# A planned attention-and-FFN kernel: new due times and engines for its copies, and slack and a lead in its plan

## The chip, the cores and the metric

One core of a Trainium2 chip runs the whole program. The metric is the device time of one execution in microseconds; lower is better. Three executions of the kernel before took 958.62, 960.18 and 961.11 us (median 960.18).

## The reference

Eight batches of eight heads, 576 positions, head size 64: causal attention over a window of 64 keys, softmax in fp32, its heads laid side by side into rows of 512; then two matrix products with a softplus between them.

```python
scores = scale * np.matmul(q, k.transpose(0, 1, 3, 2))
mask = (rel >= 0) & (rel < window)              # rel = query - key, window = 64
scores = np.where(mask, scores, -1000000000.0)
scores = scores - np.max(scores, axis=-1, keepdims=True)
attn = np.exp(scores)
attn = attn / (np.sum(attn, axis=-1, keepdims=True) + 1e-09)
x = np.matmul(attn, v)                          # -> rows of 4608 tokens x 512
...
h = x @ w_in                                    # 512 x 2048
g = np.maximum(h, 0.0) + np.log1p(np.exp(-np.abs(h)))
out = g @ w_out                                 # 2048 x 512
```

`w_in` and `w_out` come as 64-bit words, so the kernel turns them into a high and a low 32-bit part itself.

## The kernel before, in words

The 4608 tokens are cut into 12 blocks of 384 (`TB`). For each block g there are four attentions, one for each pair of heads hp (`attention(g, hp)`), and 16 FFN steps, one for each 128 columns f of the hidden layer (`ffn`). A step is an "up" (12 matmuls of 384 columns into `ps_h`, line 711), a softplus (ScalarE: Abs, Exp, Ln, lines 715 to 717; VectorE: line 723), a split of the result into a high part (line 725, on ScalarE or VectorE) and a low part (line 726, VectorE), and a "down" (9 matmuls of 512 columns that add into `ps_o`, line 735). `ps_h` and `u` have two buffers each. The steps run in a fixed order: block 0 with f = 0 to 7, block 1 with all 16, block 0 with f = 8 to 15, then blocks 2 to 11; what block 0 has summed halfway goes to DRAM and is added later.

Each f needs its weights converted once (`convert(f)`): a load of 1024 KB (line 348), "abs" on ScalarE (350), two shifts on VectorE (352, 353), a copy "hi" on ScalarE (355), and a subtraction "lo" on VectorE (356).

An attention is a chain: loads of q and k (lines 404, 405, or 435 and 439), scores on TensorE (416, or 468 and 470), a masked minimum on VectorE (389), six exponentials with sums on ScalarE (496), the reciprocal (504, 505) and the normalizing on VectorE (511). In blocks 0 and 1 the weights are then turned on TensorE (547), copied (550), multiplied with v (558) and copied and split into `x` (564, 565); from block 2 on they are split into bf16 parts (595 to 600), turned by DMA (591), multiplied (658) and gathered (665 to 670). Blocks 0 and 1 take q, k from four slots (`q_two`, `k_two`, `qk_far`) and v from `v_two`.

No engine's order is written by hand. Every operation is put in a list by `add` with its engine, a cost in us, what it depends on and what buffers it opens; `arrange` is a list scheduler in Python: again and again it takes the engine that can start earliest and there, of the operations that could start then, the one with the smallest due time. The program issues the operations in that order, and the chip runs each engine's operations in the order issued. Due times decide who goes first; no engine waits for one, only loads do: a load that opens a buffer is held in the plan until 30 us (`EARLY`) before its due time, unless it is a weight load, and while more than 4 us of transfers (`BACKLOG`) are ahead of it.

The due times come from rounds: a first guess, then for each next round the latest start that `latest` works out backward from the round before. In the last round the operations listed in `FIRST` by their number take the due time given there. Numbers follow the order of `add`: 6f to 6f+5 are load, abs, shift, shift, hi, lo of weights f; 96 to 162 are block 0's attention, 163 to 229 block 1's; 1938 and on are the FFN steps, six numbers each (up, softplus, maximum, high part, low part, down). So `FIRST` covers the first 100 us or so and not the steady part.

In the plan TensorE's costs are multiplied by `SLOW` = 1.22 for the first `COLD` = 24 us.

Of the kernel before, what the change touches and what calls it, by code (L numbers as in the profile page):

```python
# [73 lines left out]
}  # L74
DOWN = 6.3
AHEAD = (1, 1, 8, 8)
APART = (4, 6, 18, 19)
STRETCH = 1.4
COLD, SLOW = 24.0, 1.22
# [38 lines left out]
def arrange(ops, rings):  # L118
# [14 lines left out]
    while len(order) < len(ops):  # L133
        best = None
        for e, waiting in open_ops.items():
            could = []
            for o in waiting:
# [4 lines left out]
                for b in o.opens:  # L142
                    r = b.ring
                    n = len(r.taken) + taken.get(id(r), 0) - r.n
                    taken[id(r)] = taken.get(id(r), 0) + 1
                    if n >= 0:
                        users = r.taken[n].users
                        if any(id(u) not in done for u in users):
                            at = None
                            break  # L150
                        at = max([at] + [u.end for u in users])
# [24 lines left out]
        for n in o.later:  # L176
            left[id(n)] -= 1
            ready_at[id(n)] = max(ready_at[id(n)], t + cost if n.eng == o.eng and not o.nbytes else o.end)
            if not left[id(n)]:
                open_ops[n.eng].append(n)  # L180
# [44 lines left out]
def window_attention_softplus_ffn(  # L225
# [54 lines left out]

    w_raw = [buf(cpool, [P, 2, DM], w_words.dtype, "raw", tag=f"w{f}") for f in range(NF)]
# [18 lines left out]
    mask_q = att.tile([P, 3, P], BF16, name="mask_q", tag="k0")  # L300
# [8 lines left out]
    def setup():  # L309
        nc.scalar.preload_act_table_set("natural_log_exp_and_others")  # L310
        nc.gpsimd.memset(wide, 0.0)
# [26 lines left out]
    def convert(f):  # L338
# [16 lines left out]
        h = add("ACT", 1.05, lambda: nc.scalar.copy(weights(0, f), work()), deps=[a], opens=[w], uses=[work], name=f"hi{f}")  # L355
# [9 lines left out]
    def attention(g, hp):  # L365
# [27 lines left out]
        if quad:  # L393
# [27 lines left out]
            s = add("PE", 1.28, scores, deps=[lq, lk], opens=[*sp, st, mn], uses=[slot, two["q_in"], two["k_in"], *far], name=f"S{tag}")  # L421
# [8 lines left out]
        else:  # L430
# [19 lines left out]
            qn = [add("ACT", 0.4, lambda hh=hh, half=half: nc.scalar.copy(q_n()[half, :], q_in()[half, hh, :]), deps=loads[0] + before_split,  # L450
# [5 lines left out]
            for hh, half in enumerate(heads):  # L456
                k = add("DVE", 0.54, lambda hh=hh, half=half: tt(diag[0]()[half, hh, :], k_in()[half, hh, :],  # L457
# [62 lines left out]
        if by_pe:  # L520
# [21 lines left out]
            for hh in range(2):  # L542
                pp = bank()

                def turn(hh=hh, pp=pp):
                    for j in range(NJ):
                        tp(pp()[:, j * P : (j + 1) * P], sv()[:, hh * NJ + j, 0:P], ident)

                t = add("PE", 0.7, turn, deps=[nrm, t], opens=[pp] if hh else [pp, pt], uses=[st, two["xf"]], name=f"T{tag}")
                cp.append(add("ACT", 0.4, lambda hh=hh, pp=pp: nc.scalar.copy(pt()[:, hh, :], pp()[:, :TB]),  # L550
                              deps=[t], uses=[pp, pt], name=f"cp{tag}"))
            av = bank()

            def products():
# [228 lines left out]
    for f in range(NF):  # L783
        convert(f)
# [103 lines left out]
```

## Time and profile before

| | |
|---|---|
| median of three executions | 960.18 us |
| the profiled execution's own time | 959.06 us |
| its span, first to last instruction | 956.9 us |
| TensorE matmul busy | 935.2 us (98%) |
| VectorE busy | 777.7 us (81%) |
| ScalarE busy | 775.9 us (81%) |
| TensorE clock granted, mean | 0.993 |
| DMA | 117.36 MB, mean 123 GB/s |

The profiled execution lies 1.1 us under the median of the three. A span is cut into 40 slices of 23.9 us where the page shows digits; a digit is the busy share in tenths. PE is TensorE's matmuls, PEld its weight loads, DVE VectorE, ACT ScalarE, SP the engine whose queue issues most transfers. A matmul's end is modelled, so neighbouring matmuls overlap in the list: the distance from one start to the next is the better measure.

### The profile page before, as it was taken

The page shows a single profiled execution, that of the slowest core. Times are in us where ns is not written, and L with a number is a line of the kernel's source. Part 1 is how long each engine was busy: PE and PEld are TensorE (multiplying, and loading weights), DVE is VectorE, ACT ScalarE, POOL GpSimd, SP SyncE. Part 2 cuts the span into 40 slices and gives each one's busy share as a digit, 9 for nine tenths or more (in the row PEclk, how much of TensorE's full clock was granted, in tenths as well). Part 3 has the DMA queues.
Part 4 walks back from the last instruction along what each step waited for, and adds up shares of the span by engine and source line. Part 5 has one row for each costly group of instructions (what it writes and reads, how often), then busy time and mean ns, then how long its engine had stood idle before and what let it go on. Part 6 is the DMA issues. An engine that isn't in the chain of part 4 may idle for free.

```text
span 956.9 us, 16878 instructions
## 1 busy us (share of the span) xinstructions
PE 935.2 (98%) x6020; PEld 843.6 (88%) x6020; DVE 777.7 (81%) x1784; ACT 775.9 (81%) x1758; POOL 5.5 (1%) x16
## 2 busy tenths in 40 slices
PE   5999999999999999999999999999999999999998
PEld 4888988989999999998989999999999899999997
DVE  8999747898898988988888888888898888986333
ACT  7999758988888888887888888888888788877443
POOL 1000000000000000000000000000000000000000
PEclk7999999999999999999999999999999999999999
DMA  9951334565354754646346544474464633641000
GB/s 370 420 207 51 72 79 122 129 167 123 89 126 113 148 115 95 131 90 166 89 89 155 137 95 124 114 149 120 90 131 95 161 89 89 173 87 36 34 1 33
DMA packets 196675, 117.36 MB, mean 123 GB/s; under 512 B 130224, under 2 KB 187824, under 8 KB 194544
## 3 DMA queue, kind: packets, MB, share of 16 engines
q1 hardware_dynamic: 196160, 115.77, 48.2%
q8 instruction: 47, 0.77, 0.3%
q10 hardware_dynamic: 432, 0.52, 0.2%
q14 instruction: 36, 0.29, 0.1%
HBM read 74.58 MB, written 10.22 MB: 89 GB/s over the span
## 4 chain that ended last, share of the span: by engine, by line
PE 63%; ACT 15%; DVE 10%; DMA 7%; issue 3%; SPq 1%; ACTq 0%; DVEq 0%
PE ps_o L735 28%; PE ps_h L711 28%; PE ps_a L658 4%; DMA raw<-in_w_words_dram 3%; ACT st L496 2%; ACT u L716 2%; ACT u L715 2%; DMA k_in<-in_kT_dram 2%; PE ps_a L468 1%; DVE u L723 1%; PE ps_a L470 1%; DMA qk_far<-in_qT_dram 1%; DVE st L389 1%; DVE g L726 1%; DMA v_in<-in_v_dram 1%
## 5 line engine op out<-in xcount | busy, mean ns | idle before, releaser
L711 PE MATMUL ps_h<-x,w 128*128 128x384 f32 x2304 | 428.7, 337 | 2.0 <-DVE u L723 2.0
L735 PE MATMUL ps_o<-w,g 128*128 128x512 f32 x1728 | 428.5, 394 | 0.9 <-DVE g L726 0.9
L711 PEld LDWEIGHTS ps_h<-x,w 128*128 128x128 f32 x2304 | 402.6, 188 | 13.0 <-DVE u L723 3.2
L735 PEld LDWEIGHTS ps_o<-w,g 128*128 128x128 f32 x1728 | 318.2, 188 | 60.5 <-DVE g L726 1.3
L723 DVE SCALAR_TENSOR_TENSOR u<-ps_h,u 128x384 f32<-128x384 f32 x192 | 106.5, 555 | 80.5 <-ACT u L717 79.1
L496 ACT ACTIVATE st<-st,mn 128x128 f32<-128x128 f32 x288 | 111.9, 391 | 35.0 <-DVE st L488 28.9
L715 ACT ACTIVATE u<-ps_h 128x384 f32<-128x384 f32 x192 | 93.7, 488 | 45.4 <-PE ps_h L711 42.1
L726 DVE TENSOR_TENSOR g<-u,g 128x384 fp32r<-128x384 f32 x192 | 106.5, 555 | 20.9 <-ACT g L725 10.9
L717 ACT ACTIVATE u<-u 128x384 f32<-128x384 f32 x192 | 100.9, 526 | 6.1
L716 ACT ACTIVATE u<-u 128x384 f32<-128x384 f32 x192 | 100.9, 525 | 6.1
L725 ACT CAST g<-u 128x384 fp32r<-128x384 f32 x112 | 57.0, 509 | 15.5 <-DVE u L723 12.8
L658 PEld LDWEIGHTS <-v 128*128 128x128 bf16 x1136 | 55.2, 98 | 12.0 <-issue 7.7
L658 PE MATMUL ps_a<-tr,v 128*128 128x128 bf16 (+1 forms) x1136 | 64.4, 211 | 1.2 <-DVE mn L389 1.2
L665 ACT COPY xf<-ps_a 64x384 f32<-64x384 f32 x80 | 38.1, 476 | 25.9 <-PE ps_a L658 24.5
L496 ACT ACTIVATION_READ_ACCUMULATOR st<-st,mn 128x1 f32 x288 | 54.4, 189 | 0.0
L389 DVE CUSTOM_DVE_ANT_0 st<-ps_a,wide 128x192 f32<-128x192 f32 x176 | 53.9, 350 | 0.3
L619 DVE TENSOR_TENSOR v<-v_in,v 64x896 bf16<-64x896 f32 x40 | 43.5, 1088 | 9.4 <-ACT v L618 8.7
L457 DVE TENSOR_TENSOR diag<-k_in,k 64x448 fp32r<-64x448 f32 x72 | 44.4, 617 | 4.9 <-ACT k L454 3.8
L511 DVE TENSOR_TENSOR st<-st,sm 128x768 f32<-128x768 f32 x48 | 46.0, 958 | 1.6
L667 DVE TENSOR_TENSOR xf<-ps_a,xf 64x384 f32<-64x384 f32 x80 | 43.8, 547 | 3.7 <-ACT xf L665 2.1
L617 DVE TENSOR_TENSOR v_in<-v_in,v 128x896 f32<-128x896 f32 x40 | 43.5, 1086 | 2.2 <-ACT v L616 1.9
L616 ACT CAST v<-v_in 128x896 bf16<-128x896 f32 x40 | 37.3, 933 | 6.6 <-DMA v_in<-in_v_dram 6.5
(82 smaller groups left out, 834.6 us busy)
## 6 DMA issues: line engine op xcount, KB each, us to landing
v_in<-in_v_dram SPq DMA_DIRECT2D x80, 224.0 KB, 4.1
raw<-in_w_words_dram SPq DMA_DIRECT2D x16, 1024.0 KB, 13.3
k_in<-in_kT_dram SPq DMA_DIRECT2D x72, 224.0 KB, 3.7
q_in<-in_qT_dram SPq DMA_DIRECT2D x72, 192.0 KB, 4.4
out_dram<-raw SPq DMA_DIRECT2D x11, 512.0 KB, 4.0
out_dram<-raw SPq DMA_DIRECT2D x13, 256.0 KB, 2.1
v_two<-in_v_dram SPq DMA_DIRECT2D x3, 768.0 KB, 8.1
q_two<-in_qT_dram SPq DMA_DIRECT2D x8, 192.0 KB, 4.1
```

The source lines that it names most:

```text
L389: nc.vector.tensor_tensor_reduce(st()[:, hh, j, 0:width], scores, m, QSCALE, 3.0e38, ALU.add, ALU.min, mn()[:, hh, j : j + 1])
L496: nc.scalar.activation(sv()[:, i, 0:P], sv()[:, i, 0:P], AF.Exp, bias=mn()[:, hh, j : j + 1], scale=-1.0, accum_out=sm()[:, i : i + 1],)
L511: nrm = add("DVE", 0.88, lambda: tt(pn(), pn(), sm().unsqueeze(2).to_broadcast([P, 2 * NJ, P]), ALU.mult), deps=[s], uses=[st, sm], name=f ...
L658: mm(av()[:, osl], (v3() if s else v12())[:, c, hh, :, :], src, start=(i == 0), stop=(i == len(passes) - 1), skip_group_check=True,)
L711: mm(hps()[:, :TB], weight(0, a, f)[:, c * P : (c + 1) * P], x[b][c](), start=(i_mm == 0), stop=(i_mm == 3 * NC - 1))
L715: nc.scalar.activation(u(), hps()[:, :TB], AF.Abs)
L716: nc.scalar.activation(u(), u(), AF.Exp, scale=-1.0)
L717: nc.scalar.activation(u(), u(), AF.Ln, bias=1.0)
L723: m = add("DVE", 0.47, lambda: stt(u(), hps()[:, :TB], 0.0, u(), ALU.max, ALU.add), deps=[s], uses=[hps, u], name=f"m{g}.{f}")
L725: lambda: (nc.scalar.copy if by_act else nc.vector.tensor_copy)(gt[0](), u()), deps=[m], opens=[gt[0]], uses=[u], name=f"g0.{g}.{f}")
L726: lo = add("DVE", 0.47, lambda: tt(gt[1](), u(), gt[0]().bitcast(F32), ALU.subtract), deps=[h], opens=[gt[1]], uses=[u, gt[0]], name=f"g1. ...
L735: mm(acc[j](), gt[a]()[:, j * P : (j + 1) * P], weight(1, b, f), start=(first and i == 0), stop=(last and i == 2),)
```

## The change

1. `FIRST` has new numbers, now used in every round (there are eight), and covers about the same operations. The best of the rounds, by the plan's own end, is issued. Some of its due times, by operation:

| operation (number) | before | after |
|---|---|---|
| weight loads f = 0, 1, 2, 3 (0, 6, 12, 18) | 30.81, 34.09, 43.22, 57.93 | 35.86, 55.35, 61.31, 67.19 |
| block 0, pair 2: q, k (131, 132) | 34.1, 32.1 | 32.67, 31.98 |
| block 0, pair 3: q, k (147, 148) | 34.94, 34.41 | 24.25, 20.71 |
| block 0, pair 1: q (115) | 30.38 | 34.94 |
| abs f = 0 to 3 (1, 7, 13, 19) | 61.73, 47.31, 39.58, 70.35 | -179.03, -173.53, -171.58, -133.99 |
| exponentials, block 0, pairs 0 and 3 (101, 102, 152, 153) | 41.17, 34.2, 29.03, 40.19 | -104.14, 249.6, -103.86, -179 |
| exponentials, block 1 (168, 169, 186, 187, 202, 203, 218, 219) | 51.28 to 90.25 | 40.87, -4.67, -37.58, -60.21, -51.72, 206.16, -14.1, 24.06 |
| abs f = 8 to 11 (49, 55, 61, 67) | 93.65, 93.7, 100.25, 92.6 | 156.49, 204.35, -208.46, 292.06 |
| hi f = 8 to 11 (52, 58, 64, 70) | 97.07, 95.59, 110.44, 111.06 | 259.17, -179.37, 301.73, 287.09 |

2. Seventeen copies change engine (`MOVED`). From ScalarE to VectorE: "hi" of f = 0, 9, 11 (numbers 4, 58, 70); one copy of turned weights (193) and one copy into `x` (211) of block 1; the high part of five steps of block 0 (1953, 1959, 1971, 1977, 1983) and of six of block 1 (1994, 2012, 2018, 2024, 2042, 2054). From VectorE to ScalarE: one output copy of block 0's half sum (1986).
3. In the plan, after 130 us: what TensorE waits for counts as ready 0.6 us later, what comes by a transfer 2.0 us later; attention's operations get due times 5 us earlier.
4. In the plan, other costs: scores 1.28 to 0.9, turning 0.7 to 0.46, product with v 1.28 to 0.88, and smaller ones; TensorE slow by 1.6 for 4 us in place of 1.22 for 24 us.
5. Code for matmuls of zeros, which no value of the constants here lets run (`WARM` = 0), and a fourth plane of `mask_q` set to zero. The up can be cut by quarters, and is not (`CHUNKED` = 0).

```diff
+CHUNKED = 0
+MOVED = {4, 58, 70, 193, 211, 1953, 1959, 1971, 1977, 1983, 1986, 1994, 2012, 2018, 2024, 2042, 2054}
+CALM, SLACK, DMA_SLACK = 130.0, 0.6, 2.0
+WARM = 0.0
+LEAD = 5.0
-COLD, SLOW = 24.0, 1.22
+COLD, SLOW = 4.0, 1.6
...
-                        at = max([at] + [u.end for u in users])
+                        at = max([at] + [u.end + (SLACK if e == "PE" and u.end > CALM else 0.0) for u in users])
...
-            ready_at[id(n)] = max(ready_at[id(n)], t + cost if n.eng == o.eng and not o.nbytes else o.end)
+            slack = 0.0 if o.end < CALM else DMA_SLACK if o.nbytes else SLACK if n.eng == "PE" else 0.0
+            ready_at[id(n)] = max(ready_at[id(n)], t + cost if n.eng == o.eng and not o.nbytes else o.end + slack)
...
+    def move(costs, fn, default="ACT", **kw):
+        eng = default if len(ops) not in MOVED else "DVE" if default == "ACT" else "ACT"
+        do = nc.scalar.copy if eng == "ACT" else nc.vector.tensor_copy
+        o = add(eng, costs[eng == "DVE"], lambda: fn(do), **kw)
...
+        nc.vector.memset(mask_q[:, 3, :], 0.0)
...
-        h = add("ACT", 1.05, lambda: nc.scalar.copy(weights(0, f), work()), ...
+        h = move((0.95, 0.6), lambda do: do(weights(0, f), work()), ...
...
-            s = add("PE", 1.28, scores, ...
+            s = add("PE", 0.9, scores, ...
...
-                t = add("PE", 0.7, turn, ...
+                t = add("PE", 0.46, turn, ...
...
-    for r in range(ROUNDS + bool(FIRST)):
-        if r == ROUNDS:
-            for i, o in enumerate(ops):
-                o.due = FIRST.get(i, best[2][i])
+    for _ in range(ROUNDS):
+        for i, due in FIRST.items():
+            ops[i].due = due
...
-        for o in ops:
-            o.due = o.last
+        for i, o in enumerate(ops):
+            o.due = o.last - (LEAD if i in of_attention and o.last > CALM else 0.0)
...
         for o in best[1]:
+            if o.eng == "PE":
+                if o.start < WARM and o.opens:
+                    for _ in range(int((o.start - busy - 0.25) * 0.8 / 0.058)):
+                        mm(o.opens[0]()[:, 0:P], mask_q[:, 3, :], mask_q[:, 3, :], start=True, stop=True, skip_group_check=True)
+                busy = o.start + o.cost
             o.fn()
```

More of the change, by code (lines that the diff above doesn't have):

```diff
@@ L279, in add @@
         return ops[-1]
+    def move(costs, fn, default="ACT", **kw):
+        eng = default if len(ops) not in MOVED else "DVE" if default == "ACT" else "ACT"
+        do = nc.scalar.copy if eng == "ACT" else nc.vector.tensor_copy
+        o = add(eng, costs[eng == "DVE"], lambda: fn(do), **kw)
+        o.costs = costs
+        return o
     w_raw = [buf(cpool, [P, 2, DM], w_words.dtype, "raw", tag=f"w{f}") for f in range(NF)]
@@ L299, in window_attention_softplus_ffn @@
     wide, wide_c, wide_b = [cpool.tile([P, W], BF16, name=n) for n in ("wide", "wide_c", "wide_b")]
-    mask_q = att.tile([P, 3, P], BF16, name="mask_q", tag="k0")
+    mask_q = att.tile([P, 4, P], BF16, name="mask_q", tag="k0")
     ident = att.tile([P, P], F32, name="ident", tag="xf")
@@ L354, in convert @@
                 deps=[a], uses=[work, raw], name=f"c4.{f}")
-        h = add("ACT", 1.05, lambda: nc.scalar.copy(weights(0, f), work()), deps=[a], opens=[w], uses=[work], name=f"hi{f}")
+        h = move((0.95, 0.6), lambda do: do(weights(0, f), work()), deps=[a], opens=[w], uses=[work], name=f"hi{f}")
         lo = add("DVE", 1.13, lambda: tt(weights(1, f), work(), weights(0, f).bitcast(F32), ALU.subtract),
@@ L419, in scores @@
                             )
-            s = add("PE", 1.28, scores, deps=[lq, lk], opens=[*sp, st, mn], uses=[slot, two["q_in"], two["k_in"], *far], name=f"S{tag}")
+            s = add("PE", 0.9, scores, deps=[lq, lk], opens=[*sp, st, mn], uses=[slot, two["q_in"], two["k_in"], *far], name=f"S{tag}")
             scored.append(s)
@@ L449, in attention @@
                      deps=[qh], uses=[q_in, q_hl], name=f"ql{tag}")
-            qn = [add("ACT", 0.4, lambda hh=hh, half=half: nc.scalar.copy(q_n()[half, :], q_in()[half, hh, :]), deps=loads[0] + before_split,
+            qn = [add("ACT", 0.45, lambda hh=hh, half=half: nc.scalar.copy(q_n()[half, :], q_in()[half, hh, :]), deps=loads[0] + before_split,
                       opens=[] if hh else [q_n], uses=[q_in, q_n] if hh else [q_in], name=f"qn{tag}") for hh, half in enumerate(heads)]
@@ L456, in attention @@
             for hh, half in enumerate(heads):
-                k = add("DVE", 0.54, lambda hh=hh, half=half: tt(diag[0]()[half, hh, :], k_in()[half, hh, :],
+                k = add("DVE", 0.64, lambda hh=hh, half=half: tt(diag[0]()[half, hh, :], k_in()[half, hh, :],
                                                                  k_s()[half, hh, :].bitcast(F32), ALU.subtract),
@@ L547, in turn @@
                         tp(pp()[:, j * P : (j + 1) * P], sv()[:, hh * NJ + j, 0:P], ident)
-                t = add("PE", 0.7, turn, deps=[nrm, t], opens=[pp] if hh else [pp, pt], uses=[st, two["xf"]], name=f"T{tag}")
-                cp.append(add("ACT", 0.4, lambda hh=hh, pp=pp: nc.scalar.copy(pt()[:, hh, :], pp()[:, :TB]),
-                              deps=[t], uses=[pp, pt], name=f"cp{tag}"))
+                t = add("PE", 0.46, turn, deps=[nrm, t], opens=[pp] if hh else [pp, pt], uses=[st, two["xf"]], name=f"T{tag}")
+                cp.append(move((0.38, 0.47), lambda do, hh=hh, pp=pp: do(pt()[:, hh, :], pp()[:, :TB]),
+                               deps=[t], uses=[pp, pt], name=f"cp{tag}"))
             av = bank()
@@ L561, in products @@
                         )
-            pv = add("PE", 1.28, products, deps=cp + lv, opens=[av, *x_t], uses=[pt, v_now, *both], name=f"V{tag}")
-            x0 = add("ACT", 0.4, lambda: nc.scalar.copy(x_t[0](), av()[:, :TB]), deps=[pv], uses=[av, x_t[0]], name=f"x0.{tag}")
+            pv = add("PE", 0.88, products, deps=cp + lv, opens=[av, *x_t], uses=[pt, v_now, *both], name=f"V{tag}")
+            x0 = move((0.38, 0.47), lambda do: do(x_t[0](), av()[:, :TB]), deps=[pv], uses=[av, x_t[0]], name=f"x0.{tag}")
             x1 = add("DVE", 0.47, lambda: tt(x_t[1](), av()[:, :TB], x_t[0]().bitcast(F32), ALU.subtract),
@@ L705, in ffn, with up @@
         gt = [buf(ff, [P, TB], F32R, f"g{i}", n=3 - i) for i in range(2)]
-        def up():
-            i_mm = 0
-            for c in range(NC):
-                for a, b in ((0, 0), (0, 1), (1, 0)):
-                    mm(hps()[:, :TB], weight(0, a, f)[:, c * P : (c + 1) * P], x[b][c](), start=(i_mm == 0), stop=(i_mm == 3 * NC - 1))
-                    i_mm += 1
+        def up(chunks):
+            for c in chunks:
+                for i, (a, b) in enumerate(((0, 0), (0, 1), (1, 0))):
+                    mm(hps()[:, :TB], weight(0, a, f)[:, c * P : (c + 1) * P], x[b][c](), start=(c == 0 and i == 0), stop=(c == NC - 1 and i == 2))
         def soft():
@@ L717, in soft @@
             nc.scalar.activation(u(), u(), AF.Ln, bias=1.0)
-        by_act = g < 2 or f % 2
-        a = add("PE", 2.1, up, deps=[o for hp in range(NP) for o in x_ops[g, hp]] + converted[f] + ups[-1:], opens=[hps],
-                uses=[b for i in range(2) for b in x[i]] + [w_all[f]], name=f"U{g}.{f}")
+        apart = [[c] for c in range(NC)] if n < CHUNKED else [range(NC)]
+        a = ups[-1] if ups and n >= CHUNKED else None
+        for chunks in apart:
+            a = add("PE", 0.522 * len(chunks), lambda chunks=chunks: up(chunks), deps=[o for c in chunks for o in x_ops[g, c]] + converted[f] + [a],
+                    opens=[] if chunks[0] else [hps], uses=[x[i][c] for i in range(2) for c in chunks] + [w_all[f]] + ([hps] if chunks[0] else []),
+                    name=f"U{g}.{f}")
+            a.at_step = n
+        if n == CHUNKED:
+            a.deps += ups
+            for o in ups:
+                o.later.append(a)
         s = add("ACT", 1.5, soft, deps=[a], opens=[u], uses=[hps], name=f"soft{g}.{f}")
         m = add("DVE", 0.47, lambda: stt(u(), hps()[:, :TB], 0.0, u(), ALU.max, ALU.add), deps=[s], uses=[hps, u], name=f"m{g}.{f}")
-        h = add("ACT" if by_act else "DVE", 0.41 if by_act else 0.28,
-                lambda: (nc.scalar.copy if by_act else nc.vector.tensor_copy)(gt[0](), u()), deps=[m], opens=[gt[0]], uses=[u], name=f"g0.{g}.{f}")
+        h = move((0.41, 0.28), lambda do: do(gt[0](), u()), default="ACT" if g < 2 or f % 2 else "DVE", deps=[m], opens=[gt[0]], uses=[u], name=f"g0.{g}.{f}")
         lo = add("DVE", 0.47, lambda: tt(gt[1](), u(), gt[0]().bitcast(F32), ALU.subtract), deps=[h], opens=[gt[1]],
@@ L738, in down @@
                     )
-        d = add("PE", 2.075, down, deps=[h, lo, *downs[-1:]], opens=acc if first else [], uses=[*gt, w_all[f]] + ([] if first else acc), name=f"D{g}.{f}")
+        d = add("PE", 2.07, down, deps=[h, lo, *downs[-1:]], opens=acc if first else [], uses=[*gt, w_all[f]] + ([] if first else acc), name=f"D{g}.{f}")
         ups.append(a)
@@ L771, in ffn @@
                 else:
-                    c = add("ACT" if j == 1 else "DVE", 0.6,
-                            lambda view=view, j=j, j0=j0: (nc.scalar.copy if j == 1 else nc.vector.tensor_copy)(view()[:, j - j0, :], acc[j]()),
-                            deps=[d, *copies], opens=opens, uses=uses, name=f"out{g}")
+                    c = move((0.5, 0.6), lambda do, view=view, j=j, j0=j0: do(view()[:, j - j0, :], acc[j]()), default="ACT" if j == 1 else "DVE",
+                             deps=[d, *copies], opens=opens, uses=uses, name=f"out{g}")
                 copies.append(c)
@@ L784, in window_attention_softplus_ffn @@
         convert(f)
+    first_of = len(ops)
     for g in range(NB):
@@ L787, in window_attention_softplus_ffn @@
             attention(g, hp)
+    of_attention = range(first_of, len(ops))
     for n, step in enumerate(steps):
@@ L826, in window_attention_softplus_ffn @@
     dues(times)
-    for r in range(ROUNDS + bool(FIRST)):
-        if r == ROUNDS:
-            for i, o in enumerate(ops):
-                o.due = FIRST.get(i, best[2][i])
+    for _ in range(ROUNDS):
+        for i, due in FIRST.items():
+            ops[i].due = due
         for ring in rings.values():
             ring.held = [b for b in two.values() if b.ring is ring]
-        order = arrange(ops, rings)
+        try:
+            order = arrange(ops, rings)
+        except ValueError:
+            break
         end = max(o.end for o in order)
@@ L837, in window_attention_softplus_ffn @@
         latest(order, end)
-        for o in ops:
-            o.due = o.last
+        for i, o in enumerate(ops):
+            o.due = o.last - (LEAD if i in of_attention and o.last > CALM else 0.0)
     with tc.manual_schedule():
         setup()
+        busy = 1.0
         for o in best[1]:
+            if o.eng == "PE":
[3 more added lines that the diff above has]
+                busy = o.start + o.cost
             o.fn()
```

90 rows, old and new, of the table FIRST are left out of this document.

## The prediction, made before the changed kernel ran

> **What bounds the kernel now.** I read the first two parts of the profile's page, then busy time by stage, then TensorE's waits, then the start on each engine.
>
> ```profile
> span 956.9 us, 16878 instructions
> PE 935.2 (98%) x6020; PEld 843.6 (88%) x6020; DVE 777.7 (81%) x1784; ACT 775.9 (81%) x1758; POOL 5.5 (1%) x16
> ```
>
> TensorE is busy all but 21.7 us of the span. No matmul of the FFN or of attention is added or removed, so the change can only touch idle time, slow-clock time and small losses where TensorE changes from one kind of work to another. Where they lie shows by stage (columns: PE, PEld, DVE, ACT and POOL busy, granted PE clock, DMA share, GB/s):
>
> ```profile
> 0.00:30.00 30.00, 18.33 (x266) 14.90 (x267) 26.23 (x99) 24.17 (x73) 4.10 (x14) 0.77 0.96 382
> 30.00:75.00 45.00, 43.34 (x363) 37.38 (x362) 43.23 (x94) 44.45 (x107) 1.39 (x2) 1.00 0.67 275
> 75.00:100.00 25.00, 23.75 (x138) 20.74 (x137) 23.10 (x50) 22.96 (x48) 0.00 (x0) 1.00 0.21 66
> 100.00:150.00 50.00, 50.00 (x336) 44.68 (x336) 28.07 (x62) 34.06 (x79) 0.00 (x0) 1.00 0.26 64
> 150.00:875.00 725.00, 722.39 (x4517) 656.37 (x4516) 629.14 (x1428) 615.84 (x1389) 0.00 (x0) 1.00 0.53 120
> 875.00:957.00 82.00, 77.35 (x409) 69.52 (x407) 27.90 (x55) 34.46 (x68) 0.00 (x0) 1.00 0.06 20
> ```
>
> Three stages. To 100 us TensorE idles 11.67 + 1.66 + 1.25 = 14.6 us, and VectorE and ScalarE are nearly full (69.5 and 68.6 us of the first 75). From 100 to 150 us TensorE idles nothing, while VectorE has 21.9 us to spare and ScalarE 15.9: work that could have waited was done before 100 us, where both engines were the limit. From 150 to 875 us TensorE idles 2.6 us of 725. The last 4.65 us (82 less 77.35) are the end, which the change leaves alone. TensorE's waits, to 100 us and from 130 us:
>
> ```profile
> PE ps_o L416 <- DMA k_two<-in_kT_dram: 4.1, 1, 4.1
> PE ps_o L547 <- ACT st L496: 3.1, 1, 3.1
> PE ps_a L547 <- DVE sm L504: 2.2, 1, 2.2
> PE ps_h L416 <- DMA qk_far<-in_qT_dram: 1.4, 1, 1.4
> ```
>
> ```profile
> PE ps_a L658 <- DVE mn L389: 1.2, 4, 0.4
> PE ps_h L711 <- DVE u L723: 1.0, 1, 1.0
> PE ps_a L468 <- DVE xf L667: 0.3, 1, 0.3
> ```
>
> The first wait, 4.1 us for the first load, stays whatever the order. That leaves 10.5 us of idle time to 100 us and 2.5 us after 130 us.
>
> A steady step cannot become shorter by order. With nothing between, two ups take 4.16 us and three downs 6.20 us, 2.08 and 2.07 each:
>
> ```profile
> 942.00 4.16 PE ps_h L711 x24
> 946.16 6.20 PE ps_o L735 x27
> ```
>
> **The change, part by part.**
>
> *Copies that change engine.* The prices:
>
> ```profile
> L725 ACT CAST g<-u 128x384 fp32r<-128x384 f32 x112 | 57.0, 509 | 15.5 <-DVE u L723 12.8 <-PE ps_o L735 2.3
> L725 DVE CAST g<-u 128x384 fp32r<-128x384 f32 x80 | 28.7, 359 | 2.4
> L355 ACT CAST w<-work 128x1024 fp32r<-128x1024 f32 x16 | 16.6, 1049 | 1.5 <-DVE work L353 1.5
> L550 ACT COPY pt<-ps_a 128x384 f32<-128x384 f32 x12 | 5.5, 478 | 0.0
> L565 DVE TENSOR_TENSOR x<-ps_a,x 128x384 fp32r<-128x384 f32 x6 | 3.3, 548 | 0.0
> L773 DVE COPY raw<-ps_o 128x512 f32<-128x512 f32 x22 | 14.3, 683 | 0.0
> L773 ACT COPY raw<-ps_o 128x512 f32<-128x512 f32 x11 | 6.4, 578 | 0.0
> ```
>
> ScalarE loses 11 x 0.509 (high parts) + 3 x 1.049 (hi) + 2 x 0.478 (the copies of `pt` and `x`) and gains one output copy, 0.578: 9.1 us less. VectorE gains 11 x 0.359 = 3.95 us. A "hi" on VectorE has no row. VectorE's one-source pass over the same 128x1024 takes 0.708 us, its two-source pass 1.219 us (rows below); I take 0.70, by the one-source row, so 2.1 us (end 3.7). A 384-column copy out of PSUM lies between the 0.548 and the 0.683 us above; I take 0.55, so 1.1 us (end 1.4). Less the output copy's 0.68, VectorE gets 6.5 us more (end 8.4).
>
> [...]
>
> Before block 1's first up the moves take 1.05 + 5 x 0.51 + 0.95 = 4.5 us from ScalarE and give VectorE 0.70 + 5 x 0.36 + 1.1 = 3.6 us. VectorE has 5.5 us idle of its first 75 us, some of it before its first data. So alone the moves gain nothing: I put them at 0 (ends: 1 us gained, 3.6 us lost, if VectorE's chain is the longer).
>
> *Due times of the start.* What was done by 73 us:
>
> ```profile
> L711 PE MATMUL ps_h<-x,w 128*128 128x384 f32 x97 | 18.6, 342 | 0.7 <-DVE u L723 0.7
> L350 ACT ACTIVATE work<-raw 128x1024 f32<-128x1024 f32 x12 | 13.6, 1146 | 0.0
> L352 DVE TENSOR_SCALAR work<-work 128x1024 uint32<-128x1024 uint32 x12 | 8.5, 708 | 1.2 <-ACT work L350 1.2
> L353 DVE SCALAR_TENSOR_TENSOR work<-raw,work 128x1024 uint32<-128x1024 uint32 x12 | 14.6, 1219 | 0.1
> L355 ACT CAST w<-work 128x1024 fp32r<-128x1024 f32 x12 | 12.4, 1050 | 0.8 <-DVE work L353 0.8
> ```
>
> 97 up matmuls are block 0's eight ups and the first of block 1. By then twelve weights were converted, of which those eight ups need eight. The other four cost ScalarE 4 x (1.146 + 1.050) = 8.8 us and VectorE 4 x (0.708 + 2 x 1.219) = 12.6 us ("lo" at the price of line 353), which have room at 100 to 150 us. With the moves' 3.6 us set against VectorE's 12.6, the most that the start can give is 9.0 us on VectorE, and on ScalarE 8.8: 8.8 us is the ceiling. They came early because both engines fill with conversions while attention waits for its data:
>
> ```profile
> 1.66 0.42 SPq L348 DMA_DIRECT2D raw<-in_w_words_dram  x1
> ...
> 3.09 0.57 SPq L348 DMA_DIRECT2D raw<-in_w_words_dram  x1
> 3.80 0.33 SPq L405 DMA_DIRECT2D qk_far<-in_qT_dram  x1
> ```
>
> ```profile
> 12.24 1.56 PE L416 MATMUL ps_h<-qk_far 64*64 64x128 f32 x24 [1.37 <-DMA qk_far<-in_qT_dram]
> ```
>
> Two weight loads of 1.05 MB, 2.7 us each at the stage's 382 GB/s, go ahead of the q of pairs 2 and 3, and the third pair's scores wait for it until 12.24 us. The new due times put pair 3 (20.71, 24.25) and pair 2 (31.98, 32.67) ahead of weights 0 (35.86) and 1 (55.35), so these scores can start up to 5.4 us sooner. Only the q of pair 1 comes later: its due time 34.94 lets the plan load it from 4.94 us on. That exponentials come sooner does not say that everything behind them does: the new times still let ScalarE do abs of f = 0 to 3 (-179 to -134) before pair 0's exponentials (-104), and abs of f = 10 (-208) before all. So I take 3 us, a little over half of 5.4 and a third of the ceiling; ends 0 and 8.8.
>
> *Slack and lead in the plan.* They add no instruction and no wait; they change the order from 130 us on. At best they end the 2.5 us of waits there. I take 1.5 us, by the split of the list: the 1.2 us in four waits of line 658 and the 0.3 us of line 468 come from attention results that a lead brings earlier, while the 1.0 us of the up is the FFN's own chain. Ends: 2.5 us gained, and a loss priced as the third rival.
>
> *Costs, the fourth mask plane, zeros.* New costs act through the order alone (first rival's row). A memset of one plane ahead of VectorE's first copies is under 0.2 us and lies under the 4.1 us until the first scores. No matmul of zeros ran before or will: 0.
>
> **Sum.** 959.06 (the profiled execution's own time, span 956.9 and 2.2 around it) - 3.0 - 1.5 = 954.6 us. The median of the three runs is 1.1 us above that execution, so the forecast for a median is 955.7 us.
>
> **The rivals.**
>
> *The slow clock undoes the start (slower).*
>
> ```profile
> 24.02 1.55 PE L558 MATMUL ps_a<-pt,v_two 128*64 128x64 f32 x24
> 25.50 0.90 PE L547 MATMUL ps_o<-ident,st 128*128 128x128 f32 x3
> 26.33 1.56 PE L416 MATMUL ps_a<-k_two,q_two 64*64 64x128 f32 x24
> 27.82 0.96 PE L558 MATMUL ps_o<-pt,v_two 128*64 128x64 f32 x24
> 28.71 0.98 PE L416 MATMUL ps_a<-k_two,q_two 64*64 64x128 f32 x24
> 29.62 1.68 PE L711 MATMUL ps_h<-x,w 128*128 128x384 f32 x8
> ```
>
> By the distances of starts, a turn still takes 0.83 us and scores 1.49 us at 26 us (1.48 for the product, 24.02 to 25.50), and only at 27.82 is a product down to 0.89: the clock stays low for some 27 us. The old plan held scores at 1.28 x 1.22 = 1.56 until 24 us, close to the chip. The new one has 0.9, 0.46 and 0.88 after 4 us, so each pair of block 0 comes 0.59 + 2 x 0.37 + 0.60 = 1.9 us later than planned, and what is queued behind it on ScalarE and VectorE waits. If all four pairs cost these full engines that, it is 7.7 us: 959.06 - 1.5 - 3 + 7.7 = 962.3, or 963.4 as a median. It decides from 4.5 / 1.9, some two and a half pairs. Against it: the sequence is off by no more than the slip, and conversions stand between. [...]
>
> *The start is bound by the pair of engines (no change).* Both are full to 75 us, and the moves take only 4.5 - 3.6 = 0.9 us from their sum. If the four conversions are again done as filler, the first up comes sooner but block 1's does not, and the start gives nothing: 960.18 - 1.5 = 958.7. For it: even in the old list those four had later due times than block 1's exponentials, and were done.
>
> *The lead costs the FFN its place (slower).* Attention 5 us ahead puts groups of exponentials or splits before a softplus, and an up waits for `u`, like the 1.0 us wait quoted above. One such wait a block over ten blocks is 10 us: 959.06 - 3 + 10 = 966.1, as a median 967.2. It decides from five such waits. Against it: both engines are idle some 13 to 15% from 150 to 875 us, and `ps_h` has two buffers.
>
> *All of it comes.* Ceiling and all waits: 960.18 - 8.8 - 2.5 = 948.9.
>
> **Chances and range.** Forecast (951 to 957.3) 0.45; all or nearly all of it, 0.13; no change 0.24; slow clock 0.10; lead 0.08. A change under 0.3% (2.9 us) cannot be told from none here; so faster 0.58, same 0.24, slower 0.18. The range 947 to 965 goes from under the ceiling's time to just over the slow clock's, and leaves out the lead's 966 and more; the forecast's own is 951 to 957.
>
> **What would show it.** Start: scores of three pairs before 10 us, the first up (29.62 before, in the rows above) at 24 to 27 us, block 1's first up (just before 73 us now, the 97th matmul above) some 3 us sooner with fewer than twelve conversions before it, and TensorE's idle time to 100 us near 11.5. Steady part: no wait over 0.5 us after 130 us. Wrong: first up sooner but block 1's at the same time (second rival), waits on VectorE and ScalarE of 1 to 2 us before 30 us (first), ups waiting for `u` (third).

## The result and the profile after

Five executions of the changed kernel took 950.78 to 952.58 us, median 951.94; the kernel before 960.42 (median of five). The ratio is 0.9908, 95% interval 0.9894 to 0.9922: 8.5 us faster, where 4.7 was forecast on the same scale (955.7). The profiled execution took 951.15 us; its span is 7.5 us shorter (956.9 to 949.4).

The page of the changed kernel, and its busy time by stage (columns as before, without the end, from 875 us):

```profile
span 949.4 us, 16861 instructions
PE 932.0 (98%) x6020; PEld 842.1 (89%) x6020; DVE 784.7 (83%) x1800; ACT 767.7 (81%) x1743; POOL 5.0 (1%) x16
```

```profile
0.00:30.00 30.00, 19.64 (x286) 16.19 (x287) 26.74 (x103) 24.23 (x80) 4.09 (x14) 1.00 0.95 362
30.00:75.00 45.00, 44.01 (x344) 36.73 (x342) 44.07 (x98) 39.75 (x92) 0.93 (x2) 1.00 0.71 288
75.00:100.00 25.00, 24.23 (x163) 21.79 (x163) 23.69 (x58) 21.19 (x44) 0.00 (x0) 1.00 0.49 134
100.00:150.00 50.00, 49.26 (x347) 43.27 (x346) 38.88 (x84) 39.36 (x93) 0.00 (x0) 1.00 0.22 46
150.00:875.00 725.00, 725.00 (x4541) 661.27 (x4541) 627.34 (x1415) 611.80 (x1378) 0.00 (x0) 1.00 0.50 119
```

TensorE's waits to 100 us, whole. After 130 us the list has no row; the only wait between is one of 0.74 us that ends at 106.96 us.

```profile
PE ps_a L431 <- DMA k_two<-in_kT_dram: 5.7, 2, 4.6
PE ps_a L562 <- DVE st L526: 1.7, 2, 1.3
PE ps_h L431 <- DMA qk_far<-in_qT_dram: 1.4, 1, 1.4
PE ps_h L725 <- DVE u L744: 1.3, 2, 0.8
PE ps_o L562 <- DVE mn L404: 1.1, 1, 1.1
PE ps_a L573 <- ACT pt L565: 0.4, 1, 0.4
PE ps_o L562 <- DVE st L526: 0.3, 1, 0.3
```

Two gains, and not in the proportion foretold. TensorE's idle time to 100 us went from 14.6 to 12.1 us. From 150 to 875 us TensorE now runs 4541 matmuls where it ran 4517: 24 more in the same time (a rough measure, since matmuls differ in length), though TensorE idled only 2.6 us of that stretch before.

To account for all of it I took, for each group of matmuls in the trace, the distance from its start to the next group's start, less what the same group takes when nothing is in its way (an up 2.08 us, a down 2.06, a product pair 1.37). This loss, summed over groups by their start:

| loss, us | before | after |
|---|---|---|
| first matmul starts at | 4.11 | 4.61 |
| to 100 us | 21.5 | 17.0 |
| 100 to 150 us | -0.5 | 0.9 |
| 150 to 875 us | 13.9 | 8.8 |

The start gave 4.5 us less the 0.5 of its later first load, of which 1.4 came back between 100 and 150 us; the steady part gave 5.1. With 0.2 us more at the end that is the 7.5 us. The split depends on the undisturbed times: other choices from the same traces put the steady part's gain at 5 to 7 us.

### The profile page after: what moved, and what is told of

Same layout as the page of the kernel before. It is cut to its first block, busy times and chain, and to the rows that moved or that the text cites. A ratio compares the mean times of both kernels' runs of the same rounds, so it can differ in the third digit from the quotient of the medians.

```text
span 949.4 us, 16861 instructions
## 1 busy us (share of the span) xinstructions
PE 932.0 (98%) x6020; PEld 842.1 (89%) x6020; DVE 784.7 (83%) x1800; ACT 767.7 (81%) x1743; POOL 5.0 (1%) x16
## 4 chain that ended last, share of the span: by engine, by line
PE 89%; DMA 5%; DVE 4%; issue 1%; ACT 0%; SPq 0%; DVEq 0%; ACTq 0%
PE ps_o L755 39%; PE ps_h L725 39%; PE ps_a L673 6%; DMA raw<-in_w_words_dram 4%; PE ps_a L485 2%; PE ps_a L483 2%; DVE w L371 1%; DVE work L368 1%; DMA v_two<-in_v_dram 1%; DVE work L367 1%; DMA v_in<-in_v_dram 0%; DVE u L744 0%; DVE st L404 0%; DVE g L746 0%; DVE g L745 0%
## 5 line engine op out<-in xcount | busy, mean ns | idle before, releaser
L725 PE MATMUL ps_h<-x,w 128*128 128x384 f32 x2304 | 434.1, 339 | 2.0 <-DVE u L744 2.0
L745 ACT CAST g<-u 128x384 fp32r<-128x384 f32 x101 | 51.2, 507 | 11.5 <-DVE u L744 11.2
L673 PE MATMUL ps_a<-tr,v 128*128 128x128 bf16 (+1 forms) x1136 | 60.2, 211 | 0.0
L485 PEld LDWEIGHTS ps_a<-k,q_hl 128*128 128x128 f32 x216 | 39.4, 189 | 1.2
```

The source lines that it names most:

```text
L485: mm(spv[:, hh, :], q_hl()[:, hh, j * P : (j + 1) * P], k_s()[:, hh, j * P : j * P + W], start=False, stop=(hh == 1), skip_group_check=True,)
L673: mm(av()[:, osl], (v3() if s else v12())[:, c, hh, :, :], src, start=(i == 0), stop=(i == len(passes) - 1), skip_group_check=True,)
L725: mm(hps()[:, :TB], weight(0, a, f)[:, c * P : (c + 1) * P], x[b][c](), start=(c == 0 and i == 0), stop=(c == NC - 1 and i == 2))
L745: h = move((0.41, 0.28), lambda do: do(gt[0](), u()), default="ACT" if g < 2 or f % 2 else "DVE", deps=[m], opens=[gt[0]], uses=[u], name= ...
```

## The experiments

Ratios are to the kernel before on the same chip, with 95% intervals. The stretch from 150 to 875 us is read from each profile.

**1. The changed kernel without slack and lead**

```diff
-CALM, SLACK, DMA_SLACK = 130.0, 0.6, 2.0
+CALM, SLACK, DMA_SLACK = 130.0, 0.0, 0.0
-LEAD = 5.0
+LEAD = 0.0
```

> The changed kernel with SLACK, DMA_SLACK and LEAD at 0; due times, moved copies and costs as changed. Theory A (the order of the steady part gave some 5 of the 8.5 us, the start 2.5): the start stays as changed (first up near 26.2 us, block 1's first up near 70.7), the stretch from 150 to 875 us does some 24 TensorE matmuls fewer, time 956 to 958 us. Rival B (the start, and new costs of the plan, gave it all): within 1 us of 951.9.

972.17 us, 1.0116 (1.0095 to 1.0138): worse than the kernel before, where theory A said 956 to 958. Its stage row and TensorE's waits from 150 us:

```profile
150.00:875.00 725.00, 717.23 (x4455) 643.91 (x4455) 616.92 (x1407) 606.13 (x1367) 0.00 (x0) 1.00 0.50 119
```

```profile
PE ps_a L673 <- DMA tr<-nat: 6.0, 6, 1.7
PE ps_a L673 <- DVE mn L404: 0.5, 2, 0.3
PE ps_h L725 <- DVE u L744: 0.5, 2, 0.3
```

86 matmuls fewer than with slack and lead. The products with v (line 673) wait for the transfers that turn the weights, which come too late for them without slack. The list's 7.0 us are again only part of it: by start-to-start distances this stretch lost some 17 to 19 us more than the changed kernel's, about 11 of them at these products. The start is the changed one (first up 26.4, block 1's first up 71.1 us): the new due times, moves and costs without the slack and the lead make the kernel slower.

**2. The kernel before with slack and lead** (the lines of `arrange` and of the rounds that the diff shows, nothing else)

> The kernel before with SLACK 0.6, DMA_SLACK 2.0 and LEAD 5.0 alone. Theory A: start as before (first up 29.6 us, block 1's first up near 72.8), waits of TensorE after 130 us near none, time 960.4 - 5 = 955 to 956 us. Rival B: 960 us. Rival C (the lead takes the FFN's place and is only harmless with the new costs): over 962 us.

953.37 us, 0.9916 (0.9900 to 0.9931). The start is as before; the steady part has no wait of TensorE left after 150 us, and 29 matmuls more than before:

```profile
150.00:875.00 725.00, 725.00 (x4546) 660.73 (x4545) 623.79 (x1416) 615.99 (x1376) 0.00 (x0) 1.00 0.49 118
```

Theory A holds; rivals B and C fall. The interval overlaps that of the whole change: the three constants alone bring most of it.

**3. The kernel before with the new due times alone**

> The kernel before with the new FIRST table alone (used in the last round, as before; old costs, no copy moved). If the start's 2.6 us come from the due times themselves: first up near 26 us, 957 to 959 us. If they fit only the new costs and engines: the start loses what it gained or more, 960 to 964 us.

964.73 us, 1.0032 (1.0021 to 1.0043). First up at 31.0 us, block 1's first up at 75.3 us: the second outcome expected. The due times by themselves make the start worse.

**4. The changed kernel with no copy moved** (`MOVED = set()`). In its order block 3's first minima write into `st` from 132.6 us on, where block 2's split still reads at 133.8 us, so part of the computation is changed. Its 964.44 us are not the time of the same work; only its first 100 us, before any of this, are read.

> The changed kernel with MOVED empty: all copies on their default engines. My prediction priced the moves at 0 (ends: 1 us gained, 3.6 lost): 951 to 953 us, ScalarE some 9 us busier. Rival (the moves made the room at the start): ScalarE's 4.5 us before block 1's first up come back there, 955 to 957 us.

```profile
30.00:75.00 45.00, 39.13 (x305) 31.71 (x305) 43.79 (x92) 44.16 (x97) 0.93 (x2) 0.96 0.73 293
75.00:100.00 25.00, 20.60 (x123) 18.36 (x122) 22.93 (x42) 20.64 (x41) 0.00 (x0) 0.93 0.22 68
```

ScalarE is busy 44.16 us of 45 from 30 to 75 us, where the changed kernel's has 39.75 and the kernel before 44.45. TensorE loses 8.6 us of busy time to 100 us against the changed kernel, and block 1's first up is at 75.3 us, 4.6 us later: close to the 4.5 us of ScalarE that the rival named.

**5 and 6. The kernel before with SLACK alone, and with LEAD alone**

```diff
+CALM, SLACK, DMA_SLACK = 130.0, 0.6, 0.0   # 5: and LEAD = 0.0
+CALM, SLACK, DMA_SLACK = 130.0, 0.0, 0.0   # 6: and LEAD = 5.0
```

> The kernel before with SLACK 0.6 alone (no slack for transfers, no lead). Theory A1 (what the second experiment gained comes from TensorE's buffers and operands being planned 0.6 us late): 953 to 955 us, no wait of TensorE after 130 us over 0.3 us. Theory A2 (it comes from the lead): 959 to 962 us, the products still wait for VectorE's minima.

> The kernel before with LEAD 5.0 alone. Theory A1: 958 to 962 us, waits of the products for VectorE's minima as before. Theory A2: 953 to 955 us. My third rival (the lead costs the FFN its place): over 962 us, ups waiting for u.

SLACK alone: 954.03 us, 0.9930 (0.9904 to 0.9956), and no wait of TensorE at all after 130 us. LEAD alone: 959.01 us, 0.9985 (0.9975 to 0.9995), the steady part as before but for who is late. The stage row of each, and the only wait of the second after 130 us:

```profile
150.00:875.00 725.00, 725.00 (x4553) 658.67 (x4552) 628.75 (x1431) 617.78 (x1390) 0.00 (x0) 1.00 0.50 120
```

```profile
150.00:875.00 725.00, 723.18 (x4516) 655.39 (x4515) 622.93 (x1411) 613.49 (x1373) 0.00 (x0) 1.00 0.48 118
```

```profile
PE ps_a L661 <- DMA tr<-nat: 1.8, 2, 1.1
```

4553 and 4516 matmuls against 4517, and by start-to-start distances 5 to 6 us less loss with SLACK and none less with LEAD: the steady gain of this kernel is SLACK's. Theory A1 holds, A2 falls.

**7 and 12. The changed kernel with DMA_SLACK alone, and with SLACK alone**

> The changed kernel with DMA_SLACK 2.0 alone (SLACK and LEAD at 0). In the first experiment, without all three, the products waited 6.0 us for transfers of turned weights. If the slack for transfers is what the steady part of this plan needs: that wait is gone, the small waits for VectorE remain, 954 to 958 us. If it takes the lead or SLACK: 966 us or more, products waiting for the transfers as there.

> The changed kernel with SLACK 0.6 alone (DMA_SLACK and LEAD at 0). If SLACK does in the steady part what it did for the kernel before: no wait of TensorE over 0.3 us after 150 us, 4540 matmuls or more between 150 and 875 us against 4455 with none of the three, and whatever is lost against 951.9 us lies in one place between 75 and 150 us, where the order of the start meets that of the steady part. If turned weights still come late without slack for transfers: products wait for them as in the first experiment, under 4500 matmuls, 958 us or more.

DMA_SLACK alone: 958.59 us, 0.9979 (0.9969 to 0.9989). The waits for transfers are gone, and downs and ups wait for VectorE. SLACK alone: 963.26 us, 1.0033 (1.0021 to 1.0046), the other way round. TensorE's waits from 150 us, first of DMA_SLACK alone, then of SLACK alone:

```profile
PE ps_o L755 <- DVE g L745: 2.0, 7, 0.3
PE ps_h L725 <- DVE u L744: 0.7, 2, 0.6
PE ps_a L483 <- ACT u L728: 0.7, 1, 0.7
PE ps_o L755 <- DVE g L746: 0.4, 1, 0.4
```

```profile
PE ps_a L673 <- DMA tr<-nat: 3.7, 4, 1.6
PE ps_h L725 <- DVE u L744: 0.4, 1, 0.4
```

So of the two outcomes expected of the twelfth run the first, that SLACK alone clears the steady part of this plan, did not come, and the second did (with 4504 matmuls, not under 4500): the changed plan puts transfers late as well and needs the slack for both. Whether it needs the lead too is not shown; no run of it leaves out the lead alone. SLACK alone also has one down that waits 3.5 us at 106 us (below, at the eleventh run).

**8. The three hi copies back on ScalarE** (`MOVED` without 4, 58, 70)

> The changed kernel with the three hi copies back on ScalarE, the other fourteen copies moved. By price ScalarE gets 3 x 1.05 = 3.1 us more and VectorE 3 x 0.69 = 2.1 less by 100 us. If the moves matter through ScalarE's load at the start: block 1's first up 1 to 3 us later than 70.7, 953 to 955 us. If the moves are worth nothing, as I priced them: 951 to 953 us. If the due times fit only the engines they were searched with: over 957 us, lost before 100 us, with waits of ups for weights.

976.02 us, 1.0159 (1.0136 to 1.0182). Over 957 us and lost before 100 us, as the third outcome had it, but only 2.9 us of it in ups that wait for weights. Of TensorE's waits from 75 to 100 us the first row holds nearly all:

```profile
PE ps_o L755 <- DVE g L746: 12.9, 1, 12.9
```

One down waits 12.9 us for one low part (line 746), which takes 0.55 us. In VectorE's order it stands behind some twenty conversions and attention operations of block 2. It is operation 1978, whose fixed due time is 284.31, and what goes ahead of it has earlier ones. The wait also costs more than its length: the two matmuls of the down just behind it are listed with 1.22 us, the two just before it (81.66 us) with 0.73, and the mean granted clock from 75 to 100 us is 0.68, the changed kernel's 1.00. The chain of work in that stretch, its end:

```profile
92.08 0.27 DVE nat L615
...
93.61 1.14 DVE work L368
94.75 0.48 DVE g L746
...
95.27 0.80 PE ps_o L755
```

**9. Matmuls of zeros in the start** (`WARM = 28.0`)

> The changed kernel with WARM = 28, so that matmuls of zeros fill TensorE's planned idle stretches before 28 us; nothing else differs, the order of all other work is the same. In the changed kernel scores still take 1.5 us at 12 us and 0.9 at 22. If the slow clock holds up the start (my first rival's mechanism): scores take 0.9 us from about 9 us on, the first up comes 0.5 to 2 us before 26.2, and 950 to 951.5 us. If VectorE and ScalarE set the start anyway: first up within 0.3 us, 951.5 to 953 us; more if the zeros stand in the way of real work.

952.92 us, 0.9916 (0.9894 to 0.9939): no faster. TensorE in the profiled execution (954.64 us, the slowest of four; the fastest took 951.65), the first zeros, the first scores and a later turn:

```profile
1.00 4.37 PE L870 MATMUL ps_a<-mask_q 128*128 128x128 bf16 x45 [1.00 <-DVE mask_q L325]
5.29 0.89 PE L431 MATMUL ps_a<-k_two,q_two 64*64 64x128 f32 x24
...
18.54 1.49 PE L562 MATMUL ps_o<-ident,st 128*128 128x128 f32 x6
```

The scores of the first three pairs take 0.82 us from start to start, where those of the changed kernel take 1.50. It does not last: the turn at 18.54 us takes 1.49 us, the one at 11.01 us 0.83 (granted clock 0.89 in the mean to 30 us). The first up of this execution is at 30.3 us, 4 us later than without zeros. Its fourth scores start 2.4 us later (14.39 us), after 2.55 us in which TensorE waits for nothing that the profile shows; what made that is open. So this run does not settle what the slow matmuls cost.

Other profiles say a little more. In the changed kernel and in experiments 7 and 12 TensorE does the same matmuls in the same order to 100 us. The fourth scores take 1.56, 0.89 and 0.90 us there, and the first up comes at 26.21, 25.97 and 26.26 us: which of the groups are slow shows in it by 0.3 us at most.

**10 and 11. CALM 90, and LEAD 10**

> The changed kernel with CALM 90 in place of 130, so that slack and lead reach back to where the start's plan ends. The changed kernel loses 1.5 us more than the kernel before between 100 and 150 us, with one wait of 0.94 us at 104 us. If that loss is a plan without slack there: it goes, and 949.5 to 951 us. If it is what the start left undone: 951.5 to 953 us, the loss at the same place.

> The changed kernel with LEAD 10 in place of 5. My third rival (attention ahead takes the FFN's place on VectorE and ScalarE) at twice the dose: ups wait for u, 10 us lost over ten blocks, 957 to 962 us. If the lead alone is harmless: 951 to 953 us and no wait of TensorE over 0.3 us after 150 us.

CALM 90: 951.19 us, 0.9903 (0.9886 to 0.9919), not to be told from the change itself. The loss between 100 and 150 us fell from 0.9 to 0.4 us, but the start's varied by as much; the wait at 107 us is still there, with 0.34 us of 0.74. It is the fastest of my runs by median, and no better version is shown.

LEAD 10: 957.22 us, 0.9967 (0.9955 to 0.9979), in the range of the third rival but not by its mechanism. From 150 us on there is no wait and 4537 matmuls. Nearly all that is lost is at one down, from 106 us on:

```profile
PE ps_o L755 <- DVE g L746: 3.8, 1, 3.8
```

Its chain runs through block 2's attention on VectorE and ends in the low part:

```profile
108.48 0.96 DVE st L526
109.44 0.87 DVE nat L614
110.31 0.48 DVE g L746
...
110.83 3.35 PE ps_o L755 x7
```

The seven matmuls after the wait take 3.28 us from start to start, where 1.60 is usual, so the place costs 5.5 us. The mean granted clock from 100 to 150 us is 0.97, the changed kernel's 1.00.

With SLACK alone and no lead (the twelfth run) the same down at 106 us waits 3.5 us for the same line. So this wait does not need the lead. The low part is operation 2031, whose fixed due time is 332.6, while the attention ahead of it in these rows is not in `FIRST` and has due times from the rounds, all far earlier. That makes the seam of the two the likely cause; no run moved that due time.

## Why the prediction was right, and where not

*Direction and range: right.* Faster at 0.58, 951.94 us within 947 to 965 and within the forecast's own 951 to 957. The size was nearly half short, and nearly all of the shortfall is one term.

*The steady term was mis-sized, and put down to the wrong part.* "At best they end the 2.5 us of waits there" was the step that failed. Measured: 5.1 us in the profile, 6.5 us by time for SLACK alone. From 150 to 875 us the kernel before lost more than 0.2 us at nine places, 4.5 us together; the list named six waits with 2.5 us. The rows of one of them, in the kernel before:

```profile
371.38 0.85 PE L658 MATMUL ps_a<-tr,v 128*128 128x64 bf16 x14
372.65 0.85 PE L658 MATMUL ps_a<-tr,v 128*128 128x64 bf16 x14 [0.42 <-DVE mn L389]
373.34 0.42 PE L468 MATMUL ps_a<-diag,q_n 128*128 128x384 f32 x1
```

From start to start the second product takes 0.69 us and the first 1.27, so the wait cost 0.58 us; the list has 0.42, since the modelled end of a group reaches 0.16 us into the next. Every listed wait is that much too short, and shorter ones are not listed. The section on the profile before calls the distance of starts the better measure; the term was bounded by idle time all the same. In the changed kernel no place after 150 us loses more than 0.2 us; the remaining 8.8 us are spread over its 447 groups, 0.02 us each in the mean.

I gave 1.5 us to the lead. Experiments 5 and 6 give 6.5 us to SLACK and 1.5 us to LEAD by time (0.9930 and 0.9985), and the profile of LEAD alone shows no gain in the steady part. The products waited (0.42 us in the rows above) because the buffer of `ps_a` they open was still read by VectorE's minima, and SLACK counts that buffer as free 0.6 us later in the plan, so the plan puts other matmuls between. The rows of experiment 5 at about the same place have a down there, and products that wait for nothing:

```profile
371.73 2.26 PE L738 MATMUL ps_o<-w,g 128*128 128x512 f32 x9
373.83 1.52 PE L661 MATMUL ps_a<-tr,v 128*128 128x64 bf16 x28
```

*The start was right in size, for the reasons given in part.* Forecast 3 us; measured 4.0 by 100 us and 2.6 after what came back. The 3 us were a share taken between two bounds, so that they came this near is in part luck. Scores of three pairs by 10 us (4.61, 6.11, 9.05): right. First up at 26.2 us, forecast 24 to 27. Block 1's first up at 70.7 against 72.8: two of the three us. Fewer than twelve conversions before it: eight "hi" on ScalarE and one on VectorE in the changed kernel to 70.68 us:

```profile
L370 ACT CAST w<-work 128x1024 fp32r<-128x1024 f32 x8 | 8.4, 1046 | 1.3 <-DVE work L368 1.2
L370 DVE CAST w<-work 128x1024 fp32r<-128x1024 f32 x1 | 0.7, 686 | 0.0
```

The forecast put all of this down to the due times and nothing to the moves. Neither gives it alone: with the new due times and no more (experiment 3) block 1's first up is at 75.3 us, and with all but the moves (experiment 4) at 75.3 us too.

The price of a "hi" on VectorE was taken as 0.70, by the one-source row, and is 0.686 us; in the same stretch VectorE's one-source shift over 128x1024 (line 367) takes 0.687 and its two-source passes (lines 368, 371) 1.22. ScalarE's relief by the moves was computed as 4.5 us. Its busy time from 30 to 75 us fell by 4.7 (44.45 to 39.75), but that also counts conversions put off (nine "hi" on ScalarE by 75 us, twelve before), so it does not measure the moves.

*"Alone the moves gain nothing", 0 us, is not shown either way.* In this plan they cannot be taken alone: without them TensorE loses 8.6 us of busy time in the first 100 us, and three of them undone cost 24 us, 12.9 of it in one wait. Due times, costs and engines were fitted together; the price of an operation says little of what its move does to a fixed order.

*Rivals.* The slow clock: it did not undo the start. The clock was not low for some 27 us even in the kernel before, where a turn at 10.03 us took 0.84 and a product at 17.88 us 0.87: the granted clock was 0.50 from 12 to 16 us, 1.00 from 18 to 20 and 0.50 again from 22 to 26. In the changed kernel, which issues no zeros, a turn takes 1.47 us from start to start at 10.54 us and 0.85 at 14.68:

```profile
10.54 1.54 PE L562 MATMUL ps_a<-ident,st 128*128 128x128 f32 x6
12.01 1.56 PE L431 MATMUL ps_o<-k_two,q_two 64*64 64x128 f32 x24
14.68 0.85 PE L562 MATMUL ps_o<-ident,st 128*128 128x128 f32 x6 [1.12 <-DVE mn L404]
...
22.08 0.89 PE L431 MATMUL ps_a<-k_two,q_two 64*64 64x128 f32 x24
```

In the trace of the zeros the scores of the first three pairs are fast from 5.3 us on (0.82 us), and a turn at 18.54 us takes 1.49 again. No run shows what holds the clock down or brings it up. Whether a full clock all through would bring the first up sooner is not shown.

No change, as the engines are full: the start did give 4.0 us by 100 us, so no; but whether it shows in the time is open, since the whole change (0.9908) and slack and lead without the new start (0.9916) have intervals that overlap. The lead: its price, a wait of FFN work behind attention on VectorE, exists, but as one wait of 3.5 to 13 us behind a low part with a late fixed due time, not one of 1 us in each block, and also where there is no lead.

## What to carry to other kernels

When an order is fixed ahead by costs, let results count as ready a little later than the costs say wherever the busiest engine or a transfer waits on them: here 0.6 us on TensorE's side took 6.5 us off a kernel whose list of waits held 2.5. Bound what such a stretch can give by start-to-start distances against an undisturbed group, not by listed idle time. And after any change to a fitted order look first for one misplaced operation: a 0.55 us subtraction far back in VectorE's order kept TensorE waiting 13 us.

## What the runs showed of the hardware

The granted-clock column does not show the first slow stretch: it reads 1.00 for 0 to 30 us of the changed kernel, and for 12 to 14 and 22 to 24 us alone, though 24 score matmuls take 1.56 us at 12.01 us and 0.89 at 22.08 (rows above). In the kernel before it shows the next one: it reads 0.50 from 12 to 16 us, where scores take 1.49 us from start to start (12.24). That a slow clock made the first stretch too is the author's inference from equal matmuls.

One wait of TensorE cost more than its length: after 3.8 us without a matmul seven matmuls of a down took 3.28 us in place of 1.60 (experiment 11), with a mean granted clock of 0.97 from 100 to 150 us, where the changed kernel's is 1.00.
